# A new order of all engines' work, and loads issued tensor by tensor, in a recurrence with a maxout network behind it

## The chip, the cores and the metric

The kernel runs on one core of one Trainium2 chip. The metric is the device time of a run in microseconds (us); lower is better. A core has five engines with a queue of instructions each: PE (TensorE, matrix products), DVE (VectorE), ACT (ScalarE), POOL (GpSimd) and SP (SyncE, here used only to issue transfers). Each engine works through its own queue in order; an instruction whose inputs are not ready holds up everything behind it on that engine. Transfers between HBM and the on-chip memory SBUF are moved by 16 DMA engines. PE writes its products to PSUM, which has eight banks.

## The reference

Two parts follow each other. The first is a gated linear recurrence over 768 positions for 4 batches and 8 heads of size 48; the second is a network with a maximum of three products.

```python
for t in range(S):                       # S = 768, state is 48 x 48 per batch and head
    state = alpha[:, :, t, :, None] * state + np.einsum('bhd,bhe->bhde', k[:, :, t], v[:, :, t])
    y[:, :, t] = np.einsum('bhd,bhde->bhe', q[:, :, t], state)
# x: y as 3072 rows of 384
h = np.maximum(np.maximum(x @ w1, x @ w2), x @ w3)     # 384 x 768 each
out = h @ w_out                                        # 768 x 384
```

## The kernel before

The 768 positions are cut into six blocks of 128, and two batches are handled together: that makes 12 steps (0 to 11), each of 256 rows of the network. A step holds two units u (one batch each). Steps 0 and 1 are the first block of the two pairs of batches and have no state from before; steps 10 and 11 are the last block and hand no state on.

A step is written as small pieces, each a letter with an index. The pieces of one step, in the order in which data flow:

- a load of alpha, k, q and v, 384 KB each, by SP (L87), into rings of four buffers: step s + 4 reuses the buffer of step s. Weights are loaded by SP as well, in 12 parts w0 to w11 of 384 KB (L99, L102), and cast by W0 to W11 (on POOL at L140, on ACT at L138).
- N: logarithm of alpha (ACT, L168). c: sums of it by a product with a triangle (PE, L175, L178). e, f, g: exponentials of the sums (ACT, L184, L190, L196). k, q: inputs times these (POOL or DVE, L203). V: v scaled and cast (ACT, L144).
- T: transposes of q and k, eight a unit (PE, L221); t: their copy (DVE L140 or ACT L138). A: scores (PE, L235); a: scores times the mask (DVE, L248), four a step. Y: attend (PE, L271), in strips of 32 columns; x: its copy, the network's input (L138 or L140).
- S: the state's product (PE, L292); s: its sum with the old state (DVE, L304); M: gate products (POOL, L282, L284); z: the decay of the state (POOL or DVE, L309).
- G0 to G8: the network's products, six instructions of 256 columns each (PE, L322). G with index i needs weight part wi. h0 to h8: copy or maximum (h0, h3, h6 copy on ACT or DVE, L138 or L140; the others are maxima on DVE, L337). O: the output product, six of 384 columns (PE, L346); O2 to O5 are its halves, four and two products. o: scaling of the output (L144 or L146) and its store by SP (L354).
- H: fillers, products of a blank tile, which keep PE busy before the inputs have arrived (PE, L359).

What order these take is written out by hand in three strings: PROLOGUE (emitted once, with the pieces of steps 0 to 2 and the front of 3 and 4), STEADY (emitted for steps 3 to 10, in which the network of step s, the attention of step s + 1 and the sums of step s + 2 lie side by side) and LAST (step 11). "O0@-1" is piece O0 of the step before, "N0@2" piece N of the step after next. A letter behind the index names the engine (v DVE, p POOL, a ACT) or, for PE's pieces, the pool of PSUM banks that its result takes: w has two banks, s two, g four, and each pool's banks are handed out in turn, so that a piece waits until the bank's last result has been read. Each engine's queue holds its pieces in the order of the strings; nothing is reordered later.

```python
    for i, item in enumerate(LOADS.split()):       # L109: the first 28 loads, in this order
        ...
    with tc.manual_schedule():                     # L411
        ...
        emit(0, PROLOGUE)
        for s in range(3, NS):
            emit(s, LAST if s == NS - 1 else STEADY)
```

Of the kernel before, what the change touches and what calls it, by code (L numbers as in the profile page):

```python
# [23 lines left out]
def kernel(  # L24
# [14 lines left out]
    B, H, S, D = q.shape  # L39
# [42 lines left out]
    def where(s):  # L82
        return s // (B // U), (s % (B // U)) * U

    def load(n, s):
        cb, b0 = where(s)
        nc.sync.dma_start(  # L87
            rings[n][s % NQ],
            ins[n][b0:b0 + U, :, cb * P:(cb + 1) * P].rearrange("b h s d -> s (b h) d"))

    def load_step(s, *_):
        for n in "akqv":
            load(n, s)

    def load_weight(i):
        if i < 9:
# [6 lines left out]

    c16 = cpool.tile([P, 3 * P + 2], FP16, name="c16")
    c32 = cpool.tile([P, 4], FP32, name="c32")
    LOADS = """a1 a0 q0 w0 k0 k1 q1 w2 v0 a2 v1 w1
        w3 w4 w6 w5 q2 k2 w7 w8 v2 a3 w11 w10
        w9 q3 k3 v3"""
    for i, item in enumerate(LOADS.split()):  # L109
        if item[0] == "w":  # L110
            load_weight(int(item[1:]))
# [5 lines left out]
    tri, w2 = c16[:, :P], c16[:, P:P + 2]  # L117
# [8 lines left out]
    def clear_padding():  # L126
        for i in range(NQ):
            for t, eng in ((las[i], nc.vector), (qks[i], nc.gpsimd), (vts[i], nc.vector)):
                eng.memset(t.rearrange("p a b c -> p (a b) c")[:, :, D:], 0.0)
# [226 lines left out]
    def warm(_, n, *x):  # L356
# [3 lines left out]

    every, kept = NS, NS - B // U
    pieces = {
        "L": (load_step, every), "W": (cast_weight, every), "H": (warm, every), "N": (logs, every),
        "c": (sums, every), "e": (decay_in, every), "f": (decay_out, every), "g": (totals, every),
        "k": (scale_k, every), "q": (scale_q, every), "V": (values, every),
        "T": (turn, every), "t": (keep_turned, every), "A": (scores, every), "a": (masked, every),
# [5 lines left out]
    def emit(s, order):  # L372
        for piece in order.split():
            piece, _, at = piece.partition("@")
            fn, end = pieces[piece[0]]
            step = s + int(at or "0")
            if 0 <= step < end:
                i = piece[1:].rstrip("vpags")
                fn(step, int(i or 0), piece[1 + len(i):])

    PROLOGUE = """N0@1 H5@0 H2@0 H2@0 H3@0 H5@0 H1@0 H6@0 N0@0 c1@0 c0g@0 f1@0
        H4@0 c1@1 q1p@0 g0@0 f0@0 e1@0 e0@0 H4@0 q0v@0 H2@0 k1v@0 k0p@0
        c0g@1 H2@0 f0@1 q0p@1 e0@1 e1@1 T1@0 T0g@0 t1a@0 f1@1 t0@0 g0@1
        H2@0 W0a@0 H3@0 A0g@0 A1@0 H6@0 a0@0 a2@0 V0@0 a1@0 a3@0 k0p@1
        k1v@1 H2@0 H2@0 T0@1 N0@2 L0@4 H2@0 q1p@1 T1g@1 Y0@0 Y1@0 t0@1
        A0@1 H2@0 t1@1 x0v@0 x1@0 V0@1 W2p@0 A1g@1 S1@0 a0@1 a1@1 a3@1
        c1@2 G0@0 e1@2 c0@2 f0@2 H2@0 a2@1 f1@2 S0@0 e0@2 Y0g@1 g0@2
        h0v@0 Y1g@1 W3a@0 s1a@0 W1p@0 W6p@0 G1@0 x1v@1 x0v@1 W4a@0 G2@0 h1@0
        s0@0 G0@1 h0@1 S1@1 G1@1 G3@1 h2@0 S0@1 M0@0 h1@1 W5a@0 s0@1
        G3@0 z0p@0 z1p@0 q1p@2 G4@0 G2@1 h3@0 h3v@1 L0@5 G4@1 h4@0 q0v@2  # L390
        h2@1 G6@0 G5@1 k1p@2 k0v@2 T0@2 h4@1 s1a@1 T1g@2 h6@0 t0a@2 W7p@0
        h5@1 t1@2 G5@0 G6@1 W8a@0 A0g@2 A1@2 h5@0 a0@2 G7@0 h6@1 W11p@0
        G8@0 G7@1 W10p@0 a1@2 W9p@0 V0@2 a2@2 a3@2 Y0@2 h7@1 N0@3 Y1@2
        G8@1 c1@3 x0@2 h7@0 h8@0 c0@3 h8@1 x1@2 f0@3 f1@3 G0@2 G1@2
        G2@2 q1p@3 e0@3 G3@2 q0p@3 h0@2 h3@2 h1@2 h2@2 G4@2 g0@3 k0p@3
        O0@0 e1@3 o0v@0 M0@1 L0@6 G6@2 h4@2 O1@0 k1v@3 G5@2 o1@0 h6v@2
        T0@3 t0a@3 T1g@3 O0@1 h5@2 t1@3 o0v@1 A0@3 V0@3 A1g@3 z0p@1 a2@3
        O1g@1 a3@3 a0@3 a1@3 N0@4 c1g@4 G7@2 o1@1 g0@4 z1p@1 G8@2 M0@2
        e1@4 h7@2 c0g@4 k1p@4 f1@4 f0@4 e0@4 Y0@3 Y1g@3 q0p@4 q1v@4 h8@2
        x0@3 x1@3 V0@4 k0v@4"""  # L400
    STEADY = """S1@-1 S0g@-1 N0@2 T1@1 t1@1 s0@-1 s1@-1 O0@-1 T0@1 G0@0 t0@1 G3@0
        z0v@-1 A1@1 a2@1 A0g@1 z1p@-1 O1@-1 o0v@-1 h0@0 a0@1 c0@2 h3@0 G1@0
        c1g@2 e0@2 a1@1 f0@2 G2@0 a3@1 e1@2 g0@2 G4@0 k1p@2 o1@-1 Y0@1
        h1@0 h2@0 h4@0 f1@2 q0p@2 k0p@2 V0@2 Y1@1 G5@0 h5@0 x0@1 G6@0
        q1p@2 x1@1 G7@0 L0@4 h6v@0 h7@0 G8@0 M0@0 h8@0"""
    LAST = """G0@0 G3@0 h0@0 G1@0 h1@0 h3@0 G2@0 G6@0 h2@0 h6@0 G7@0 G5@0
        G4@0 G8@0 h7@0 O0@-1 h4@0 h5@0 h8@0 O1g@-1 o0v@-1 O4g@0 O5@0 O2g@0
        o1@-1 O3@0 o1v@0 o0@0"""

    blank = cpool.tile([P, 512], FP16, name="blank")  # L410
    with tc.manual_schedule():  # L411
        nc.vector.memset(blank, 0.0)  # L412
        clear_padding()
# [4 lines that stand above are left out]
# [29 lines left out]
```

## Time and profile before

| | |
|---|---|
| median of 5 runs | 159.64 us (159.06 to 160.28) |
| the profiled execution, time | 159.64 us |
| its span, first to last instruction | 157.9 us |
| granted PE clock, mean | 0.996 |
| busy: PE, DVE, ACT, POOL | 150.7, 126.6, 78.7, 62.0 us |
| transfers | 28.73 MB, mean 182 GB/s |
| first piece of the first steady step (S1@2) starts | 54.17 us |
| the last step's PE work (LAST) begins | 144.6 us |
| last output product ends | 154.45 us |

Times in the text are microseconds from the span's start. In a list of instruction groups a line reads: line of the code, engine, operation, output<-input with shapes and types, number of instructions, busy time and mean duration in ns, and the idle time of the engine just ahead of them with what ended it. A timeline's line reads: start, length, engine, line, operation, tiles, shapes, number of instructions merged, and in brackets the idle time ahead and what ended it. PE's instructions overlap each other: what one costs is the time from its start to the next start, and its listed length is longer.

### The profile page before, as it was taken

The numbers are of one execution on the slowest core, as the hardware profiler recorded it, in microseconds if no ns is written. First come the engines' busy times: TensorE is split into PE (matmuls) and PEld (weight loads), VectorE is DVE, ScalarE is ACT, GpSimd is POOL, SyncE is SP. The second block draws the span as 40 slices with busy tenths as digits, with TensorE's granted clock in tenths as the row PEclk, the third lists the DMA queues.
The fourth block names the chain that finished last, engine by engine and source line by source line (L and its number), as shares of the span: only waits on it lengthen the run. The fifth ranks groups of instructions, "written<-read, shape, count | busy, mean of one in ns | idle before, by whom it ended". The sixth has DMA issues, their size and how long they took to land.

```text
span 157.9 us, 4886 instructions
## 1 busy us (share of the span) xinstructions
PE 150.7 (95%) x2057; PEld 115.1 (73%) x2057; DVE 126.6 (80%) x210; ACT 78.7 (50%) x153; POOL 62.0 (39%) x87
## 2 busy tenths in 40 slices
PE   6999998979998999999999999999999999999991
PEld 2355667868865777878878878878878879778860
DVE  3024997799667799899898998998998998998570
ACT  3447368557636739628329249059067164222211
POOL 5024802950585623724625427328319219200000
PEclk9999999999999999999999999999999999999998
DMA  5999999999899999999899999999981011020014
GB/s 121 214 262 247 183 269 338 202 294 282 223 198 211 222 172 240 209 235 303 179 228 218 224 220 226 228 232 218 229 183 56 0 50 54 0 104 2 4 50 150
DMA packets 107254, 28.73 MB, mean 182 GB/s; under 512 B 99808, under 2 KB 107232, under 8 KB 107232
## 3 DMA queue, kind: packets, MB, share of 16 engines
q1 hardware_dynamic: 106944, 28.32, 81.9%
q8 instruction: 16, 0.26, 0.7%
q10 hardware_dynamic: 288, 0.10, 0.2%
q14 instruction: 6, 0.05, 0.1%
HBM read 23.69 MB, written 4.72 MB: 180 GB/s over the span
## 4 chain that ended last, share of the span: by engine, by line
PE 67%; SPq 13%; DMA 8%; DVE 5%; ACT 3%; issue 1%
PE gps L322 39%; PE ops L346 12%; SPq L87 9%; PE yps L271 5%; PE tps L221 4%; DMA ws<-in_moe_w_dram 4%; SPq L99 4%; DMA ra<-in_alpha_dram 4%; PE aps L235 3%; PE lps L175 2%; DVE qk L203 2%; PE sps L292 2%; ACT h L138 1%; PE lps L178 1%; DVE hT L337 1%
## 5 line engine op out<-in xcount | busy, mean ns | idle before, releaser
L322 PE MATMUL gps<-xT,wcat 128*128 128x256 f16 x648 | 77.8, 273 | 0.8 <-POOL wcat L140 0.6
L322 PEld LDWEIGHTS <-wcat 128*128 128x128 f16 x648 | 61.3, 98 | 10.1 <-POOL wcat L140 0.8
L248 DVE TENSOR_TENSOR lat<-aps,c 128x512 f16<-128x512 f32 x48 | 30.6, 683 | 0.8 <-PE aps L235 0.7
L138 ACT CAST h<-gps 128x512 f16<-128x512 f32 x25 | 14.5, 586 | 32.7 <-PE gps L322 32.1
L203 POOL TENSOR_TENSOR qk<-rk,ic 128x384 f16<-128x384 f32 x19 | 19.8, 1041 | 25.4 <-ACT ge L196 20.8
L337 DVE TENSOR_TENSOR h<-gps,h 128x512 f16<-128x512 f32 x36 | 24.6, 685 | 5.8 <-ACT h L138 2.6
L337 DVE TENSOR_TENSOR hT<-gps,h 128x512 f16<-128x512 f32 x36 | 24.7, 690 | 5.4 <-PE gps L322 3.3
L346 PE MATMUL ops<-wo,hT 128*128 128x384 f16 x144 | 26.9, 326 | 0.0
L203 POOL TENSOR_TENSOR qk<-rq,ac 128x384 f16<-128x384 f32 x21 | 21.4, 1023 | 10.6 <-ACT ge L196 7.4
L346 PEld LDWEIGHTS <-hT 128*128 128x128 f16 x144 | 13.0, 98 | 7.8 <-issue 0.2
L309 POOL TENSOR_TENSOR st<-full,gm 128x384 f16<-128x384 f32 x12 | 9.9, 830 | 20.7 <-DVE full L304 20.6
L359 PE MATMUL wps<-blank 128*128 128x512 f16 x57 | 16.3, 433 | 1.2 <-DVE blank L412 1.2
L140 DVE COPY qkT<-tps 128x1024 f16<-128x1024 f16 x21 | 14.3, 683 | 2.2 <-PE tps L221 2.2
L184 ACT ACTIVATE ic<-lps 128x384 f32<-128x384 f32 x24 | 11.6, 493 | 8.6 <-PE lps L175 7.6
L221 PE MATMUL tps<-c,qk 128*128 128x128 f16 x192 | 14.5, 219 | 1.3 <-DVE qk L203 0.8
L168 ACT ACTIVATE la<-ra 128x768 f16<-128x768 f32 x12 | 10.3, 860 | 10.8 <-DMA ra<-in_alpha_dram 10.8
L221 PEld LDWEIGHTS <-qk 128*128 128x128 f16 x192 | 12.0, 97 | 3.5 <-DVE qk L203 1.2
L190 ACT ACTIVATE ac<-lps 128x384 f32<-128x384 f32 x24 | 11.6, 495 | 4.2 <-PE lps L175 2.5
L144 ACT ACTIVATE vt<-rv,c 128x768 f16<-128x768 f32 x12 | 11.4, 946 | 4.3 <-DMA rv<-in_v_dram 4.3
L359 PEld LDWEIGHTS <-blank 128*128 128x128 f16 x57 | 5.8, 109 | 8.2 <-issue 3.3
L144 ACT ACTIVATE ob<-ops,c 128x384 f32<-128x384 f32 x12 | 7.0, 584 | 8.8 <-PE ops L346 8.8
L271 PE MATMUL yps<-lat,vt 128*32 128x128 f16 x384 | 10.3, 219 | 0.0
(37 smaller groups left out, 141.0 us busy)
## 6 DMA issues: line engine op xcount, KB each, us to landing
ra<-in_alpha_dram SPq DMA_DIRECT2D x12, 384.0 KB, 4.9
rq<-in_q_dram SPq DMA_DIRECT2D x12, 384.0 KB, 5.9
rk<-in_k_dram SPq DMA_DIRECT2D x12, 384.0 KB, 5.8
rv<-in_v_dram SPq DMA_DIRECT2D x12, 384.0 KB, 6.0
out_dram<-ob SPq DMA_DIRECT2D x24, 192.0 KB, 2.6
ws<-in_moe_w_dram SPq DMA_DIRECT2D x9, 384.0 KB, 5.0
ws<-in_moe_w_out_dram SPq DMA_DIRECT2D x3, 384.0 KB, 6.2
c<-c ACTq DMA_DIRECT2D x1, 96.5 KB, 3.0
```

The source lines that it names most:

```text
L87: nc.sync.dma_start(rings[n][s % NQ], ins[n][b0:b0 + U, :, cb * P:(cb + 1) * P].rearrange("b h s d -> s (b h) d"))
L138: nc.scalar.copy(out=dst, in_=src)
L140: engines[eng].tensor_copy(out=dst, in_=src)
L144: nc.scalar.mul(dst, src, col)
L203: engines[eng or "p"].tensor_mul(dst.rearrange("p a b c -> p (a b) c")[:, :, :D], src[:, u * H:(u + 1) * H], dec)
L221: nc.tensor.transpose(tps[:, i, p, :], qk[:, u * NP + i * HP + p].rearrange("p a b -> p (a b)"), ident)
L248: nc.vector.tensor_mul(lat, aps_of[s, u][i], m)
L271: nc.tensor.matmul(yps[C * c:C * (c + 1), f, :], job[n][0], job[n][1], start=(n == 0), stop=(n == len(job) - 1))
L322: nc.tensor.matmul(gps[:, j, :], wcat[:, f, g, jj * P:(jj + 1) * P], xT[:, f].rearrange("p u t -> p (u t)"), start=(f == 0), stop=(f == NF ...
L337: nc.vector.tensor_max(h, gps, h_of[s, i - 1])
L346: nc.tensor.matmul(ops, hT_of[s][:, jj, u * P:(u + 1) * P], wo16[:, jj, :], start=(jj == 0), stop=(jj == NJ - 1))
L359: nc.tensor.matmul(wps, blank[:, :P], blank, start=True, stop=True)
```

## The change

All three order strings and the order of the first loads are new. Loads of later steps, which were one piece L that issued alpha, k, q and v, become four pieces l0 to l3 that issue one tensor each. The pieces themselves, the tiles, the banks and the buffers are unchanged; which engine or bank pool a piece uses is changed for some of them by its letter. In STEADY, the copy t1 goes from DVE to ACT, h0 from ACT to DVE, h6 from DVE to ACT, the decay z0 from DVE to POOL, k0 from POOL to DVE, V from ACT to DVE; the scores' pair A0 A1, the attend pair Y0 Y1 stay adjacent on PE, O0 goes to the front of the step, and the loads go ahead of the store of o1.

```diff
--- before.py
+++ after.py
@@ -88,9 +88,8 @@
             rings[n][s % NQ],
             ins[n][b0:b0 + U, :, cb * P:(cb + 1) * P].rearrange("b h s d -> s (b h) d"))
 
-    def load_step(s, *_):
-        for n in "akqv":
-            load(n, s)
+    def load_step(s, i, _):
+        load("akqv"[i], s)
 
     def load_weight(i):
         if i < 9:
@@ -103,9 +102,9 @@
 
     c16 = cpool.tile([P, 3 * P + 2], FP16, name="c16")
     c32 = cpool.tile([P, 4], FP32, name="c32")
-    LOADS = """a1 a0 q0 w0 k0 k1 q1 w2 v0 a2 v1 w1
-        w3 w4 w6 w5 q2 k2 w7 w8 v2 a3 w11 w10
-        w9 q3 k3 v3"""
+    LOADS = """a0 a1 k0 q0 q1 k1 v0 v1 a2 w0 w1 w3
+        w2 k2 q2 w4 w6 w5 w7 w8 v2 a3 w10 w9
+        w11 q3 k3 v3"""
     for i, item in enumerate(LOADS.split()):
         if item[0] == "w":
             load_weight(int(item[1:]))
@@ -360,7 +359,7 @@
 
     every, kept = NS, NS - B // U
     pieces = {
-        "L": (load_step, every), "W": (cast_weight, every), "H": (warm, every), "N": (logs, every),
+        "l": (load_step, every), "W": (cast_weight, every), "H": (warm, every), "N": (logs, every),
         "c": (sums, every), "e": (decay_in, every), "f": (decay_out, every), "g": (totals, every),
         "k": (scale_k, every), "q": (scale_q, every), "V": (values, every),
         "T": (turn, every), "t": (keep_turned, every), "A": (scores, every), "a": (masked, every),
@@ -378,34 +377,35 @@
                 i = piece[1:].rstrip("vpags")
                 fn(step, int(i or 0), piece[1 + len(i):])
 
-    PROLOGUE = """N0@1 H5@0 H2@0 H2@0 H3@0 H5@0 H1@0 H6@0 N0@0 c1@0 c0g@0 f1@0
-        H4@0 c1@1 q1p@0 g0@0 f0@0 e1@0 e0@0 H4@0 q0v@0 H2@0 k1v@0 k0p@0
-        c0g@1 H2@0 f0@1 q0p@1 e0@1 e1@1 T1@0 T0g@0 t1a@0 f1@1 t0@0 g0@1
-        H2@0 W0a@0 H3@0 A0g@0 A1@0 H6@0 a0@0 a2@0 V0@0 a1@0 a3@0 k0p@1
-        k1v@1 H2@0 H2@0 T0@1 N0@2 L0@4 H2@0 q1p@1 T1g@1 Y0@0 Y1@0 t0@1
-        A0@1 H2@0 t1@1 x0v@0 x1@0 V0@1 W2p@0 A1g@1 S1@0 a0@1 a1@1 a3@1
-        c1@2 G0@0 e1@2 c0@2 f0@2 H2@0 a2@1 f1@2 S0@0 e0@2 Y0g@1 g0@2
-        h0v@0 Y1g@1 W3a@0 s1a@0 W1p@0 W6p@0 G1@0 x1v@1 x0v@1 W4a@0 G2@0 h1@0
-        s0@0 G0@1 h0@1 S1@1 G1@1 G3@1 h2@0 S0@1 M0@0 h1@1 W5a@0 s0@1
-        G3@0 z0p@0 z1p@0 q1p@2 G4@0 G2@1 h3@0 h3v@1 L0@5 G4@1 h4@0 q0v@2
-        h2@1 G6@0 G5@1 k1p@2 k0v@2 T0@2 h4@1 s1a@1 T1g@2 h6@0 t0a@2 W7p@0
-        h5@1 t1@2 G5@0 G6@1 W8a@0 A0g@2 A1@2 h5@0 a0@2 G7@0 h6@1 W11p@0
-        G8@0 G7@1 W10p@0 a1@2 W9p@0 V0@2 a2@2 a3@2 Y0@2 h7@1 N0@3 Y1@2
-        G8@1 c1@3 x0@2 h7@0 h8@0 c0@3 h8@1 x1@2 f0@3 f1@3 G0@2 G1@2
-        G2@2 q1p@3 e0@3 G3@2 q0p@3 h0@2 h3@2 h1@2 h2@2 G4@2 g0@3 k0p@3
-        O0@0 e1@3 o0v@0 M0@1 L0@6 G6@2 h4@2 O1@0 k1v@3 G5@2 o1@0 h6v@2
-        T0@3 t0a@3 T1g@3 O0@1 h5@2 t1@3 o0v@1 A0@3 V0@3 A1g@3 z0p@1 a2@3
-        O1g@1 a3@3 a0@3 a1@3 N0@4 c1g@4 G7@2 o1@1 g0@4 z1p@1 G8@2 M0@2
-        e1@4 h7@2 c0g@4 k1p@4 f1@4 f0@4 e0@4 Y0@3 Y1g@3 q0p@4 q1v@4 h8@2
-        x0@3 x1@3 V0@4 k0v@4"""
-    STEADY = """S1@-1 S0g@-1 N0@2 T1@1 t1@1 s0@-1 s1@-1 O0@-1 T0@1 G0@0 t0@1 G3@0
-        z0v@-1 A1@1 a2@1 A0g@1 z1p@-1 O1@-1 o0v@-1 h0@0 a0@1 c0@2 h3@0 G1@0
-        c1g@2 e0@2 a1@1 f0@2 G2@0 a3@1 e1@2 g0@2 G4@0 k1p@2 o1@-1 Y0@1
-        h1@0 h2@0 h4@0 f1@2 q0p@2 k0p@2 V0@2 Y1@1 G5@0 h5@0 x0@1 G6@0
-        q1p@2 x1@1 G7@0 L0@4 h6v@0 h7@0 G8@0 M0@0 h8@0"""
-    LAST = """G0@0 G3@0 h0@0 G1@0 h1@0 h3@0 G2@0 G6@0 h2@0 h6@0 G7@0 G5@0
-        G4@0 G8@0 h7@0 O0@-1 h4@0 h5@0 h8@0 O1g@-1 o0v@-1 O4g@0 O5@0 O2g@0
-        o1@-1 O3@0 o1v@0 o0@0"""
+    PROLOGUE = """N0@0 N0@1 H2@0 H9@0 H2@0 H2@0 H1@0 H3@0 H2@0 c0@0 c1@1 c1g@0
+        e1@0 f1@0 H2@0 k1p@0 f0@0 H3@0 q1v@0 g0@0 e0@0 H1@0 H1@0 T1@0
+        H1@0 q0v@0 H1@0 k0p@0 c0g@1 g0@1 f1@1 H4@0 e1@1 f0@1 t1@0 q1v@1
+        H2@0 q0v@1 e0@1 T0@0 H4@0 k0p@1 H2@0 A1g@0 a2@0 k1p@1 T0g@1 T1@1
+        t0a@0 V0@0 a3@0 t0@1 t1a@1 l0@4 l1@4 l2@4 l3@4 A0g@0 N0@2 a0@0
+        H4@0 W3p@0 W1p@0 W6p@0 A1g@1 W5p@0 a1@0 A0@1 a2@1 a0@1 a1@1 H2@0
+        a3@1 S1@0 S0@0 H1@0 s1@0 H5@0 c1@2 V0@1 Y0g@1 W0v@0 Y0@0 Y1g@1
+        c0@2 x0@0 x1v@1 S1g@1 x0@1 s0a@0 Y1g@0 l0@5 l1@5 l2@5 l3@5 x1v@0
+        f0@2 s1@1 g0@2 G0@1 h0v@1 H3@0 W7p@0 G0@0 h0@0 G1@1 e1@2 M0@0
+        W8p@0 W2v@0 G3@0 G1@0 h1@1 f1@2 e0@2 k1v@2 k0v@2 G2@0 h1@0 h3@0
+        S0@1 W4a@0 q1v@2 q0v@2 G3@1 G2@1 z0p@0 z1p@0 W9p@0 W11p@0 h2@0 T1@2
+        h3@1 t1a@2 T0@2 h2@1 G4@0 G4@1 h4@0 G6@0 t0a@2 h4@1 G6@1 s0@1
+        A1@2 G5@1 h6v@1 h6@0 G5@0 V0@2 a3@2 a2@2 h5@1 h5@0 G7@0 A0@2
+        G8@0 a0@2 G7@1 a1@2 h7@0 Y1@2 Y0@2 x0@2 x1v@2 N0@3 h8@0 G8@1
+        G0@2 G1@2 c1@3 h7@1 h0@2 h8@1 g0@3 h1@2 G2@2 c0@3 f0@3 e0@3
+        e1@3 W10p@0 G6@2 q0p@3 M0@1 G4@2 G3@2 h2@2 f1@3 h3@2 h4@2 G5@2
+        q1v@3 h6@2 k0v@3 h5@2 k1p@3 O0@0 O0g@1 T0@3 t0a@3 T1g@3 z1p@1 o0v@1
+        V0@3 t1@3 l0@6 l1@6 l2@6 l3@6 O1@0 o1@0 A1@3 A0g@3 G8@2 o0v@0
+        O1@1 a3@3 a1@3 N0@4 G7@2 a2@3 c1@4 a0@3 h7@2 z0p@1 o1v@1 c0g@4
+        f1@4 h8@2 Y1@3 Y0g@3 g0@4 M0@2 e0@4 f0@4 e1@4 x1v@3 q0v@4 k0v@4
+        q1p@4 x0@3 V0@4 k1v@4"""
+    STEADY = """O0@-1 S1g@-1 G0@0 s1@-1 G1@0 S0@-1 T0@1 T1@1 h0v@0 t0@1 h1@0 o0v@-1
+        G3@0 G6@0 t1a@1 s0@-1 A0g@1 N0@2 A1@1 h3@0 O1@-1 h6@0 z1p@-1 a1@1
+        z0p@-1 G2@0 a0@1 G4@0 c0g@2 l0@4 l1@4 l2@4 l3@4 a2@1 h2@0 h4@0
+        a3@1 c1@2 G7@0 e0@2 G8@0 k0v@2 e1@2 G5@0 f1@2 f0@2 h7@0 g0@2
+        q1p@2 o1@-1 Y0@1 Y1g@1 x0@1 q0p@2 k1p@2 x1@1 h5@0 h8@0 V0v@2 M0@0"""
+    LAST = """O0@-1 G0@0 G3@0 h3v@0 G4@0 G5@0 h4@0 h0@0 G6@0 h6@0 G1@0 h5@0
+        G7@0 G2@0 h1@0 h7@0 h2@0 G8@0 h8@0 O1@-1 O4g@0 o1@-1 O5g@0 O2g@0
+        o0v@-1 O3@0 o1@0 o0@0"""
 
     blank = cpool.tile([P, 512], FP16, name="blank")
     with tc.manual_schedule():
```

## The prediction

> **What bounds the kernel now.** I read the page first, then a table of stages, then the matrix engine's (PE) timeline, then the waits on loads. The profiled execution took 159.64 us, which is also the median; its span is 157.9 us, so 1.74 us lie around the span. All sums below are made against this execution.
>
> ```profile
> PE 150.7 (95%) x2057; PEld 115.1 (73%) x2057; DVE 126.6 (80%) x210; ACT 78.7 (50%) x153; POOL 62.0 (39%) x87
> ...
> q8 instruction: 16, 0.26, 0.7%
> ...
> L359 PE MATMUL wps<-blank 128*128 128x512 f16 x57 | 16.3, 433 | 1.2 <-DVE blank L412 1.2
> ```
>
> PE is busy for 95% of the span, and 57 of its instructions are fillers on a blank tile. The table of stages, two steady steps and the last stretch (columns: stretch, length, busy time and count of PE, PEld, DVE, ACT, POOL, granted clock, DMA share, GB/s):
>
> ```profile
> 77.55:88.81 11.26, 11.26 (x176) 9.15 (x174) 10.49 (x18) 6.06 (x13) 5.08 (x8) 1.00 1.09 225
> 88.81:100.07 11.26, 11.26 (x176) 9.15 (x174) 10.49 (x18) 5.78 (x12) 5.08 (x8) 1.00 1.10 223
> 144.60:157.90 13.30, 9.81 (x79) 7.39 (x76) 6.24 (x10) 2.92 (x5) 0.00 (x0) 0.95 0.17 60
> ```
>
> A steady step is 11.26 us of PE with nothing idle, at full clock; DVE has 0.77 us to spare in it. Is anything hidden in those 11.26 us? The PE timeline of a step, read by differences of starts:
>
> ```profile
> 102.12 1.47 PE L322 MATMUL gps<-xT,wcat 128*128 128x256 f16 x12
> 103.53 0.62 PE L235 MATMUL aps<-qkT 48*128 48x128 f16 x16
> 104.08 1.15 PE L346 MATMUL ops<-wo,hT 128*128 128x384 f16 x6
> ...
> 108.55 2.79 PE L322 MATMUL gps<-xT,wcat 128*128 128x256 f16 x24
> 111.18 0.50 PE L292 MATMUL sps<-vt,qk 128*128 128x96 f16 x8
> ```
>
> 24 gate products take 111.18 - 108.55 = 2.63 us, 0.109 each. The 12 ahead of the scores take 1.41, 0.10 more than 12 x 0.109: the change of array shape. There are four such changes in a step (into and out of scores, into and out of attend), 0.4 us. No other hole shows. So only the prologue, up to the first steady step at 54.17, has waits to lose.
>
> ```profile
> 32.32 0.39 PE L221 MATMUL tps<-c,qk 128*128 128x128 f16 x4
> 33.51 0.84 PE L221 MATMUL tps<-c,qk 128*128 128x128 f16 x12 [0.80 <-DVE qk L203]
> ...
> 47.01 0.39 PE L221 MATMUL tps<-c,qk 128*128 128x128 f16 x4
> 47.78 0.84 PE L221 MATMUL tps<-c,qk 128*128 128x128 f16 x12 [0.39 <-POOL qk L203]
> ```
>
> Four transposes last 4 x 0.057 = 0.23, so the first pair of lines hides 33.51 - 32.55 = 0.96 us, the second 47.78 - 47.24 = 0.54. By the same reading the other losses are 0.5 (15.1), 0.3 (21.2), 0.77 (23.9), 0.2 (43.5), 0.28 (51.0) in the prologue, 0.25 (54.5) and 0.31 (59.8) in the first steady step: about 4 us. That is the most that any order could win, since the change keeps all work.
>
> What holds the prologue's end is the loads. Timelines of ACT, DVE and POOL:
>
> ```profile
> 46.31 0.56 DVE L203 TENSOR_TENSOR qk<-rk,ic 128x384 f16<-128x384 f32 x1 [0.17 <-DMA rk<-in_k_dram]
> ...
> 46.35 1.38 POOL L203 TENSOR_TENSOR qk<-rk,ic 128x384 f16<-128x384 f32 x1 [0.15 <-DMA rk<-in_k_dram]
> ...
> 50.45 0.84 ACT L168 ACTIVATE la<-ra 128x768 f16<-128x768 f32 x1 [0.39 <-DMA ra<-in_alpha_dram]
> ...
> 58.80 0.84 ACT L168 ACTIVATE la<-ra 128x768 f16<-128x768 f32 x1 [1.98 <-DMA ra<-in_alpha_dram]
> ```
>
> k of step 3 lands at 46.3, alpha of step 4 at 50.4, alpha of step 5 at 58.8, and the stages above show a DMA share of 1.0 and more. The queue is the limit, so the nth load lands when it does whatever the engines' order.
>
> **The change: what stays.** I counted the pieces of both orders: prologue, steady step and last step hold the same pieces, 57 fillers included. Steady PE work and its four changes of shape are the same (A0 A1 adjacent, Y0 Y1 adjacent). So are the last step's 54 gate and 24 projection products; it moves O0@-1 ahead of the gates, 6 x 0.163 us, a shift within PE. I cost it at nothing: h8@0 still has O1 and O4 (0.97 + 0.65 us) to hide behind, of which it needs about 0.9. The last output still goes over ACT (0.58) and then its store. Loads split by tensor stay a, k, q, v in a row on SP: the split itself is 0. In a steady step they now stand ahead of the store of o1 rather than behind it; the DMA share is full until 118 us, and a steady step asks for its alpha some 3 us after landing (94.9 against 98.1, step 9), so 0.
>
> **The first loads.** The 20 first loads are the same set in both orders and the 8 after them end q3 k3 v3 in both, with only weights w9 to w11 turned. So k3 at 46.3 and a4 at 50.4 stay. Within the 20, attention's inputs come earlier (v1 about 17.0 in place of 22.2, by 1.7 us a load) and w0 at about 20.3 in place of 9.8.
>
> **The front, to G0@1.** PE: fillers start at 1.19, 12 of them cold until 6.28, 9 more at 0.215 to 8.21; sums 0.90, 7 fillers 1.5: 10.6. T1@0 waits for q1@0: q0 lands at about 10.1, DVE shares the multiply's time with POOL's k1@0 (as at 10.4 now, 1.00 us) and ends at 11.3: 0.7 us lost. Then T 0.46, 2 fillers, c 0.16, 6 fillers, T 0.46, 6 fillers: scores A1g@0 at 15.4. From there DVE is the chain: from 15.9 eight masks and one transposed copy at 0.61 each, 0.2 us of waiting for A1g@1 in between, to 21.65; s1@0 0.5; cast W0v, new on DVE, between 0.4 (half its time on ACT, 0.84) and 0.9, I take 0.8, the near row; x1@1 0.5: G0@1 starts at 23.6.
>
> **To the k3 gate.** From G0@1 to T0@3 PE has 25 gate pieces x 0.655 = 16.4, 3 fillers 0.65, S 0.17, T@2 0.91, A@2 apart and so with two more changes of shape 0.96, Y@2 1.0, c@3 0.53, O0 twice 1.95: 22.6 us, hence 46.15. I held each gate against its weight: G4@0 at 30.6 (w4 at 28.9 + 0.84), G8@0 at 36.1 (w8 at 34.7 + 0.83), Y1@2 at 37.4 (v2 at 36.45 + 0.94, a tenth late). The 0.96 us before T@2 goes, since k2 and q2 land some 4 us earlier. But now k3 decides: k0v@3 on DVE is done at 46.87, k1p@3 on POOL at 47.73 (the two rows above are this very pair). T0@3 goes at 46.9, T1g@3 at 47.8. What was won ahead, up to 1.2 us, is waited away here.
>
> **From the gate to the first steady step.** After 47.8: T1 0.46, O1@0 0.97, A@3 0.65, G8@2 0.66, O1@1 0.97, G7@2 0.66, c@4 0.53, Y@3 1.0: 5.9, so 53.7. Now it takes from 47.78 to 54.17. a4 does not bind: its logarithm ends at 51.3, c1@4 comes at 52.2. Gain **0.47**.
>
> **First steady step.** N@5 stands ahead of h3@3 and h6@3 on ACT. If a5 lands at 58.8, h3 ends at 60.25 and G2@3, due at 60.15, is 0.1 late. On DVE x1@3, q0@4, k0@4, k1@4 and s1 push h1@3 to about 59.0; A0g@4, due at 58.65, needs its bank: 0.3. Together 0.4, where now 0.56 are lost: gain 0.16.
>
> **Steady steps.** DVE gives up t1 (0.6) and z0 (0.83) and takes k0 (0.56 alone, 1.21 beside POOL) and V (0.4 to 0.9). I walked it from step start: h1 4.5 (needed by A0g at 4.94), o0 5.0 (O1 at 5.49), a0 6.8 (c0g at 7.78), k0v 9.14, h7 9.70, h5 10.41, h8 11.02 to 11.71. The next O0, now first in the step, reads h8's half in its fifth product at 11.27 + 0.65 = 11.92. Cover 0.15 us: nothing lost. Here a rule of the Trainium skill speaks against the change: SBUF — State Buffer, section "SBUF: two separate sides", says that a vector operation with two SBUF inputs and a GpSimd operation hold a common port pair exclusively, the later one blocked to the end. The 1.38 us on POOL beside DVE's 0.56 above (1.00 alone) agrees in kind. By the rows, k0v starts at 9.14, ahead of POOL's q1 at 9.4, and takes 0.56: sum 0. By the rule with POOL first, k0v waits up to 1.0, less the cover: up to 0.85 us in each of seven steps, 6 us. I take the row, since q1p waits for f1, which ACT makes after e0. V is last on DVE; if blocked behind k1p for 1.0 it still ends before t0 is due.
>
> **Sum.** -0.47 - 0.16 + 0 = -0.63: 159.64 - 0.63 = **159.0 us**.
>
> **Rivals and chances.** Within 0.5% (158.84 to 160.44) counts as no change, about what a measurement of this kernel can tell. (A) As above, 158.4 to 159.5, chance 0.45; two fifths of it below 158.84. (B) The gates ease: k3 half a microsecond sooner, no loss in the first steady step, 159.0 - 0.5 - 0.4 = 158.1; for it, alpha 5's late landing is one row; against it, the full DMA share; 0.20. (C) The front slips by more than the 1.2 us of slack at k3, DVE's row of masks being the place; 1.5 us beyond the slack would give 160.5, a small slip about 159.6; 0.17, a third of it slower. (D) Slower: h8 comes after O0's fifth product in every step, by DVE's k0v beside POOL. It decides from 0.15 us on; at 1.21 us for k0v it costs 0.65 - 0.15 = 0.5 in seven steps, 3.5 us: 162.5; 0.18. That PE's fetches matter and the new order frees them, I count in B: 16 blocks are moved and no hole in a step answers to them. Faster 0.18 + 0.20 = 0.38, same 0.27 + 0.12 = 0.39, slower 0.05 + 0.18 = 0.23. The range, 157.9 to 161.5, takes in B and C and D's lower part.
>
> **What would show it.** T1g@3 of the new profile resumes near 47.8 after POOL; the first steady O0@2 near 53.7; steady steps 11.26 us with O0 unbroken; G0@1 near 23.6. I am wrong if a steady step is longer than 11.3, if k3 lands elsewhere than 46 to 46.7, or if PE reaches T0@3 after 47.3.

## The result, and the profile after

The changed kernel took 158.74 us (median of 28 runs, 158.27 its lowest) against 159.79 us before (49 runs). The ratio is 0.9948, 95% interval 0.9931 to 0.9965: a gain of 0.83 us, 0.56 to 1.10. I had said 159.0 us, a gain of 0.63. On two other occasions the same kernel was set beside the one before and the ratio was 0.9919 (0.9892 to 0.9946) and 0.9900 (0.9852 to 0.9948), gains of 1.3 and 1.6 us: the gain is real. The three intervals overlap, so that it was larger on those occasions is not shown.

The profile that came with the result ran at a granted clock of 0.855 and a span of 172.5 us, so the profiles read here are those of the same kernel at full clock from the experiments: run 11 (span 156.6 us), unless another is named. Stages of it, two steady steps and the last stretch, in the columns used above (PE, PEld, DVE, ACT, POOL, granted clock, DMA share, GB/s):

```profile
77.29:88.56 11.27, 11.27 (x177) 9.16 (x175) 10.68 (x18) 5.76 (x12) 5.40 (x8) 1.00 0.99 204
88.56:99.82 11.26, 11.26 (x176) 9.16 (x174) 10.68 (x18) 5.76 (x12) 5.39 (x8) 1.00 1.03 221
143.20:156.60 13.40, 9.97 (x86) 7.55 (x78) 5.69 (x9) 3.52 (x7) 0.00 (x0) 1.00 0.16 60
```

A steady step is 11.26 us of PE as before: the new order gains nothing there. DVE is at 10.68 rather than 10.49 us. Next comes the gate at k3, by which I mean the place where PE can go no further until k of step 3 has landed (a "gate piece" is something else, one of G0 to G8). The timelines of PE, DVE and POOL there:

```profile
46.51 1.13 PE L220 MATMUL tps<-c,qk 128*128 128x128 f16 x12
47.87 0.40 PE L220 MATMUL tps<-c,qk 128*128 128x128 f16 x4 [0.24 <-POOL qk L202]
...
46.40 0.56 DVE L202 TENSOR_TENSOR qk<-rk,ic 128x384 f16<-128x384 f32 x1 [0.53 <-DMA rk<-in_k_dram]
...
46.51 1.30 POOL L202 TENSOR_TENSOR qk<-rk,ic 128x384 f16<-128x384 f32 x1 [1.13 <-DMA rk<-in_k_dram]
```

PE comes to the transposes at 46.5, k3 lands at 46.4, DVE's multiply ends at 46.96, POOL's at 47.81, and the last four transposes go at 47.87. Sixteen transposes need 0.91 us and take from 46.51 to 48.11: 0.69 us are waited away. What follows, in PE's timeline (the first steady step) and DVE's:

```profile
53.57 1.14 PE L345 MATMUL ops<-wo,hT 128*128 128x384 f16 x6
54.54 0.33 PE L291 MATMUL sps<-vt,qk 128*128 128x96 f16 x4
54.77 1.47 PE L321 MATMUL gps<-xT,wcat 128*128 128x256 f16 x12
56.07 0.33 PE L291 MATMUL sps<-vt,qk 128*128 128x96 f16 x4
56.24 1.06 PE L220 MATMUL tps<-c,qk 128*128 128x128 f16 x16
57.14 1.47 PE L321 MATMUL gps<-xT,wcat 128*128 128x256 f16 x12
58.54 0.62 PE L234 MATMUL aps<-qkT 48*128 48x128 f16 x16
...
64.87 1.15 PE L345 MATMUL ops<-wo,hT 128*128 128x384 f16 x6
...
54.49 0.70 DVE L202 TENSOR_TENSOR qk<-rq,ac 128x384 f16<-128x384 f32 x1
55.12 1.01 DVE L202 TENSOR_TENSOR qk<-rk,ic 128x384 f16<-128x384 f32 x2
56.06 0.54 DVE L303 TENSOR_TENSOR full<-sps,st 128x384 f32<-128x384 f32 x1
56.52 0.67 DVE L139 CAST h<-gps 128x512 f16<-128x512 f32 x1
57.12 0.67 DVE L139 COPY qkT<-tps 128x1024 f16<-128x1024 f16 x1
57.72 0.67 DVE L336 TENSOR_TENSOR h<-gps,h 128x512 f16<-128x512 f32 x1
```

The first steady step starts at 53.57 (54.17 before) and has no wait worth naming on PE: each row begins where the row ahead of it has issued its last product, and only 0.06 us are lost at S1. The next step starts at 64.87, so this one took 11.30 us. In the profile of before PE's timeline of the first steady step, up to the start of the next, has

```profile
54.17 0.51 PE L292 MATMUL sps<-vt,qk 128*128 128x96 f16 x8
54.77 0.62 PE L221 MATMUL tps<-c,qk 128*128 128x128 f16 x8
...
58.06 0.72 PE L235 MATMUL aps<-qkT 48*128 48x128 f16 x16
58.71 1.15 PE L346 MATMUL ops<-wo,hT 128*128 128x384 f16 x6
59.69 0.33 PE L175 MATMUL lps<-la,c 128*128 128x384 f16 x1
60.16 0.81 PE L322 MATMUL gps<-xT,wcat 128*128 128x256 f16 x6
...
66.11 0.50 PE L292 MATMUL sps<-vt,qk 128*128 128x96 f16 x8
```

and took 66.11 - 54.17 = 11.94 us: 0.25 are lost ahead of T1, 0.1 within the scores and 0.31 ahead of a gate piece.

Where did the 1.24 us between the two spans (157.86 and 156.62) come from? 0.60 are gained by the start of the first steady step (54.17 against 53.57) and 0.64 within that step (11.94 against 11.30). Behind it nothing changed: from the second steady step to the last product's start it is 154.08 - 66.11 = 87.97 us before and 152.84 - 64.87 = 87.97 now, and from there to the span's end both take 3.78.

### The profile page after: what moved, and what is told of

Read it like the earlier page. It is cut to its first block, busy times and chain, and to the rows that moved or that the text cites. A ratio compares the mean times of both kernels' runs of the same rounds, so it can differ in the third digit from the quotient of the medians.

```text
span 172.5 us, 4881 instructions
## 1 busy us (share of the span) xinstructions
PE 167.4 (97%) x2057; PEld 122.2 (71%) x2057; DVE 130.1 (75%) x215; ACT 77.9 (45%) x150; POOL 60.3 (35%) x85
## 4 chain that ended last, share of the span: by engine, by line
PE 91%; DMA 3%; SPq 2%; DVE 1%; ACT 0%; issue 0%; DVEq 0%
PE gps L321 47%; PE ops L345 17%; PE tps L220 7%; PE yps L270 6%; PE wps L358 4%; PE aps L234 4%; DMA rq<-in_q_dram 3%; PE lps L174 2%; SPq L87 2%; PE sps L291 2%; PE lps L177 1%; DVE qk L202 1%; ACT ob L143 0%; DVEq L202 0%
## 5 line engine op out<-in xcount | busy, mean ns | idle before, releaser
L321 PE MATMUL gps<-xT,wcat 128*128 128x256 f16 x648 | 88.2, 294 | 0.0
L321 PEld LDWEIGHTS <-wcat 128*128 128x128 f16 x648 | 65.1, 103 | 14.5
L345 PE MATMUL ops<-wo,hT 128*128 128x384 f16 x144 | 30.4, 355 | 0.0
L137 ACT COPY qkT<-tps 128x1024 f16<-128x1024 f16 x13 | 13.1, 1013 | 32.5 <-PE tps L220 32.5
L308 POOL TENSOR_TENSOR st<-full,gm 128x384 f16<-128x384 f32 x20 | 16.9, 847 | 28.8 <-DVE full L303 23.7
L202 POOL TENSOR_TENSOR qk<-rq,ac 128x384 f16<-128x384 f32 x16 | 16.5, 1049 | 26.6 <-ACT ac L189 26.6
L137 ACT CAST xT<-yps 128x384 f16<-128x384 f32 x20 | 9.2, 482 | 14.7 <-PE yps L270 14.7
L202 POOL TENSOR_TENSOR qk<-rk,ic 128x384 f16<-128x384 f32 x12 | 12.0, 1003 | 9.4 <-ACT ic L183 7.2
L139 DVE COPY qkT<-tps 128x1024 f16<-128x1024 f16 x11 | 7.6, 688 | 5.5 <-PE tps L220 5.5
L202 DVE TENSOR_TENSOR qk<-rq,ac 128x384 f16<-128x384 f32 x8 | 5.6, 725 | 8.1 <-DMA rq<-in_q_dram 8.1
```

The lines of the kernel that those rows point to most:

```text
L137: nc.scalar.copy(out=dst, in_=src)
L202: engines[eng or "p"].tensor_mul(dst.rearrange("p a b c -> p (a b) c")[:, :, :D], src[:, u * H:(u + 1) * H], dec)
L308: engines[eng or "p"].tensor_mul(sts[b0 + u][(cb + 1) % 2].rearrange("p a (b d) -> p a b d", d=D), full_of.pop((s, u)), gm_of[s][:, u * HP ...
L321: nc.tensor.matmul(gps[:, j, :], wcat[:, f, g, jj * P:(jj + 1) * P], xT[:, f].rearrange("p u t -> p (u t)"), start=(f == 0), stop=(f == NF ...
L345: nc.tensor.matmul(ops, hT_of[s][:, jj, u * P:(u + 1) * P], wo16[:, jj, :], start=(jj == 0), stop=(jj == NJ - 1))
```

## The experiments

All ratios are against the kernel before, run on the same chip. Runs 1 to 4, 5 to 8 and 9 to 11 went together, and medians are compared within such a group or through these ratios.

**1, the changed kernel as it is.**

> The changed kernel as it is, for a profile at full clock. Both theories: about 0.8 us under the kernel before. Load gate: T1g@3 resumes at 47.8 after POOL's k1@3, the first steady O0@2 starts near 53.7, steady steps are 11.26 us. Steady order (rival): the first steady step starts near 54.2 as before and the gain comes behind it.

Measured: 159.05 us, ratio 0.9919 (0.9892 to 0.9946). k3 landed at 46.94, 0.56 us later than in run 11; the last four transposes of T1@3 went on at 48.43, and the first steady step started at 54.13, not at 53.7. Shift these by the late landing and they stand about where they were expected. But from there on PE lost only 0.06 us. So both answers were half right in this execution: with a late k3 the start is no sooner than in the old profile, and the gain lies behind it.

**2 and 3, the two halves alone.** Run 2 has the new LOADS and PROLOGUE (together the new front) with the old STEADY and LAST; run 3 the reverse.

```diff
 # run 2: changed kernel, with
+    STEADY = """S1@-1 S0g@-1 N0@2 T1@1 t1@1 s0@-1 s1@-1 O0@-1 T0@1 G0@0 ...   (old)
+    LAST = """G0@0 G3@0 h0@0 G1@0 h1@0 ...   (old)
 # run 3: changed kernel, with
+    LOADS = """a1 a0 q0 w0 k0 k1 q1 w2 v0 a2 v1 w1 ...   (old)
+    PROLOGUE = """N0@1 H5@0 H2@0 H2@0 H3@0 ...   (old)
```

> New LOADS and PROLOGUE, old STEADY and LAST. Load gate: 0.5 to 0.8 us under the kernel before, about the time of the changed kernel. Steady order: 0 against the kernel before.

> Old LOADS and PROLOGUE, new STEADY and LAST. Load gate: 0 to 0.2 us under the kernel before. Steady order: 0.6 to 0.8 us under it.

Measured: run 2 160.78 us, ratio 1.0046 (1.0018 to 1.0073); run 3 160.05 us, ratio 0.9979 (0.9952 to 1.0006). Neither theory had this: the new front alone is slower, the new steady order alone is not told apart from no change, both together gain 0.8%. The seam between them is the place. PE's timeline of run 2 at its first steady step:

```profile
55.21 0.50 PE L295 MATMUL sps<-vt,qk 128*128 128x96 f16 x8
56.42 0.40 PE L224 MATMUL tps<-c,qk 128*128 128x128 f16 x4 [0.72 <-POOL qk L206]
57.78 0.40 PE L224 MATMUL tps<-c,qk 128*128 128x128 f16 x4 [0.95 <-DVE qk L206]
58.01 1.14 PE L349 MATMUL ops<-wo,hT 128*128 128x384 f16 x6
```

The old step begins with T1@4 after 0.34 us, and the new front leaves k1 of step 4 to the end of DVE's queue: about 2.0 us are lost, 0.87 ahead of the first transposes (56.42 - 55.55) and 1.13 between the eight of them (58.01 - 56.42, less the 0.46 that they need). In run 3 the new step begins with O0, and the old front leaves h8@2 behind q1@4 on DVE:

```profile
55.17 0.82 PE L349 MATMUL ops<-wo,hT 128*128 128x384 f16 x4
56.54 0.50 PE L349 MATMUL ops<-wo,hT 128*128 128x384 f16 x2 [0.54 <-DVE hT L340]
```

O0's fifth product waits for h8, 0.72 us. That is the kind of wait that the slower rival (D) of the prediction had in each step, here once at the seam; its cause is another, h8's place in DVE's queue and not a k0v held up by POOL. Later steps are 11.27 us in both runs.

**4, five more fillers ahead of c1@2.**

```diff
-H1@0 s1@0 H5@0 c1@2
+H1@0 s1@0 H10@0 c1@2
```

> The changed kernel with five more fillers (1.07 us of PE) ahead of c1@2. Load gate: PE reaches T0@3 up to 1.2 us ahead of k3, so 0 to 0.3 us over the changed kernel. Rival, PE's own work sets the end of the prologue: 1.07 us over it.

Measured: 159.17 us, ratio 0.9936 (0.9904 to 0.9969), 0.12 us over run 1, which is not told apart from none. It tells less than I had meant: the fillers went into a wait that stood just there (0.41 + 0.47 us in run 1, for alpha 2 and for V1 behind it), so PE came to G0@1 at 24.21 as in run 1 (24.25), and the slack at k3 was not touched.

**5, the kernel before once more.**

> The kernel before once more, for a second profile beside those of the changed kernel, to see how far a load's landing moves from one execution to the next. Load gate: T1 and T0 of step 3 resume within 0.6 us after k3 lands, wherever that is, and the first steady step loses 0.5 to 1 us. Rival (the order alone sets it): the first steady step starts at 54.2 again whatever k3 does.

Measured: 160.8 us in this one execution, span 159.0. The first steady step starts at 55.12, not 54.17, and takes 12.15 us, 0.9 more than a later one; 0.78 of that is a wait at T1@4. k3 landed at 47.28, but PE did not wait for it: alpha 3, late at 40.6, had held PE already. PE's timeline of this run, and that of run 6, which has the new front and an alpha 3 as late (40.4):

```profile
39.44 0.83 PE L322 MATMUL gps<-xT,wcat 128*128 128x256 f16 x6
41.51 0.32 PE L175 MATMUL lps<-la,c 128*128 128x384 f16 x1 [1.25 <-ACT la L168]
```

```profile
39.82 2.14 PE L321 MATMUL gps<-xT,wcat 128*128 128x256 f16 x18
41.80 0.33 PE L174 MATMUL lps<-la,c 128*128 128x384 f16 x1
```

The old order has c1@3 behind one gate piece (G8@1) and waits; the new one has G0@2 and G1@2 between and does not. My expectation that k3 would rule the old kernel as well was wrong for this execution. It doesn't follow that the new front fares better with late loads: in run 6 k3 landed at 48.10 and the first steady step started at 55.29, no sooner than here.

**6, the transposes early in the steady step.**

```diff
-O0@-1 S1g@-1 G0@0 s1@-1 G1@0 S0@-1 T0@1 T1@1 h0v@0
+O0@-1 S1g@-1 T0@1 T1@1 G0@0 s1@-1 G1@0 S0@-1 h0v@0
```

> The changed kernel with the transposes T0@1 T1@1 of the steady step moved ahead of G0 G1 S0, near where the old order has them. If the gain is the late place of the transposes in the first steady step: 0.9 to 1.1 us over the changed kernel, all of it in the first steady step, waiting for q and k of step 4 on DVE; later steps 11.26 us. Rival (their place doesn't matter): 0.

Measured: 160.0 us, ratio 0.9963 (0.9932 to 0.9995), where run 7 beside it, equal to the changed kernel in time, has 0.9918 (0.9891 to 0.9945): by the ratios some 0.7 us lost, though the intervals just overlap. The profile decides it: it has 0.49 + 0.25 us of waiting for DVE's q and k in the first steady step, which takes 12.02 us instead of 11.30, and a later one takes 11.27. This move alone gives back more than half of the gain.

**7, five more fillers behind G0@1.**

```diff
-G0@1 h0v@1 H3@0 W7p@0
+G0@1 h0v@1 H8@0 W7p@0
```

> The changed kernel with five more fillers (1.07 us of PE) between G0@1 and G0@0, behind the wait for alpha 2 that took in the five of the earlier run. Load gate at k3: PE reaches T0@3 at 47.7 rather than 46.7 and waits the less: 0 to 0.3 us over the changed kernel. Rival, PE's work sets the end: 1.07 us over it.

Measured: 159.25 us, ratio 0.9918. Against run 1 (0.9919) the 1.07 us of PE work cost nothing that shows; the ratio is good to 0.4 us. PE's timeline at the gate, with k3 at 47.10:

```profile
47.02 0.39 PE L220 MATMUL tps<-c,qk 128*128 128x128 f16 x4
47.74 0.62 PE L220 MATMUL tps<-c,qk 128*128 128x128 f16 x8 [0.34 <-DVE qk L202]
48.59 0.40 PE L220 MATMUL tps<-c,qk 128*128 128x128 f16 x4 [0.23 <-POOL qk L202]
```

With 1.07 us more work ahead of it PE still waits 0.5 us and then 0.4 here, though k3 also came 0.7 us later than in run 11.

**8 and 9, k3 loaded first.** Both load q3 and k3 ahead of the output weight, cast that weight behind k1@3 on POOL and put the output products behind the scores; run 9 also mends two places in DVE's queue. Stretches left out are marked by dots.

```diff
 # run 8
-v2 a3 w10 w9 w11 q3 k3 v3
+v2 a3 q3 k3 w10 w9 w11 v3
-q1v@3 h6@2 k0v@3 h5@2 k1p@3 O0@0 O0g@1 T0@3 t0a@3 T1g@3 ... A1@3 A0g@3 G8@2 ... O1@1 ... G7@2
+q1v@3 h6@2 k0v@3 h5@2 k1p@3 W10p@0 W9p@0 W11p@0 T0@3 t0a@3 T1g@3 ... G7@2 h7@2 G8@2 h8@2
+V0@3 A1@3 A0g@3 a3@3 a1@3 a2@3 a0@3 O0@0 O0g@1 o0v@0 ... O1@0 O1@1 o0v@1 N0@4 c1@4 o1@0
 # run 9, besides
-f1@3 h3@2 h4@2 G5@2 q1v@3 h6@2 k0v@3 h5@2
+f1@3 k0v@3 q1v@3 h3@2 h4@2 G5@2 h6@2 h5@2
-a3@3 a1@3 a2@3 a0@3 O0@0 O0g@1 o0v@0
+a3@3 a1@3 O0@0 o0v@0 a2@3 a0@3 O0g@1
```

> The changed kernel with q3 and k3 loaded ahead of the three parts of the output weight, and T, G7, G8, A of step 3 ahead of the four output products that need these. Load gate: k3 lands near 43.5, the waits at T@3 (1.1 us) go, the first steady step starts near 53.1: 0.6 to 1.0 us under the changed kernel. Rival (another gate, alpha 4 or q4 k4, stands just behind): 0 to 0.3 us under it.

Measured: 161.83 us, ratio 1.0077 (1.0052 to 1.0102). k3 landed at 42.5, four us sooner, and T@3 waited longer than ever. PE's timeline, and DVE's:

```profile
47.51 0.84 PE L220 MATMUL tps<-c,qk 128*128 128x128 f16 x12 [2.50 <-DVE qk L202]
...
44.79 0.69 DVE L336 TENSOR_TENSOR h<-gps,h 128x512 f16<-128x512 f32 x1 [2.05 <-ACT h L137]
45.40 0.97 DVE L202 TENSOR_TENSOR qk<-rq,ac 128x384 f16<-128x384 f32 x1
46.29 1.17 DVE L202 TENSOR_TENSOR qk<-rk,ic 128x384 f16<-128x384 f32 x1
```

h4@2 stood at the head of DVE's queue for 2.05 us waiting for ACT's h3; the multiplies were behind it, and then beside POOL's casts took 0.97 and 1.17 us, where the changed kernel has 0.55 and 0.56. (The profiled execution, at 160.91, is one of the faster ones: seven of the twelve had a mean clock of 0.989 instead of 0.997 and took 161.75 to 162.3. Where their clock fell is not on record, so part of the median's loss stays open.)

> As the run with k3 first, but k0 and q1 of step 3 moved on DVE ahead of h4@2, where DVE sat idle for 2.05 us waiting for ACT's h3, and o0@0 ahead of two masks. If that run lost its 2.7 us at T@3 to DVE's queue: T@3 runs without a wait, the first steady step starts near 53.2, 0.5 to 1.0 us under the changed kernel. Rival (the loads set the end in some other place, alpha 4, q4 or alpha 5): the time of the changed kernel within 0.3 us.

Measured: 158.58 us, ratio 0.9888 (0.9841 to 0.9934), beside 158.92 and 0.9900 for run 11: the wait of 2.7 us is gone, which puts it down to DVE's queue, but the 0.3 us under the changed kernel is not told apart from none. Another wait took the gate's place:

```profile
44.65 0.83 PE L220 MATMUL tps<-c,qk 128*128 128x128 f16 x12
45.77 0.40 PE L220 MATMUL tps<-c,qk 128*128 128x128 f16 x4 [0.29 <-POOL qk L202]
```

0.45 us go to POOL's k1@3, which stands behind q0@3 and the gate products M on POOL, and the first steady step starts at 53.40, against 53.57 in run 11 and 53.2 expected.

**10, the old LOADS under the new order.** Only the list of loads is the old one.

```diff
-    LOADS = """a0 a1 k0 q0 q1 k1 v0 v1 a2 w0 w1 w3 w2 k2 q2 w4 w6 w5 w7 w8 ...
+    LOADS = """a1 a0 q0 w0 k0 k1 q1 w2 v0 a2 v1 w1 w3 w4 w6 w5 q2 k2 w7 w8 ...
```

> The changed kernel with the old LOADS. v1 lands 5 us later and attend of step 1 waits for it, weights 0, 1 and 2 come earlier. Load gate at k3, which stays in its place, with PE some 1 to 2 us ahead of it: 0 to 0.4 us over the changed kernel. Rival (the earlier inputs of the attention are the gain): 0.8 us or more over it.

Measured: 166.45 us, ratio 1.0355 (1.0304 to 1.0405). I had looked at v1 alone. It cost 0.9 us, as G0@1 came at 24.97 against 24.07 in run 11; most of the rest is one wait for q2 and k2 and the slower clock behind it. PE's and DVE's timelines, and two stages (columns as above):

```profile
35.78 1.89 PE L220 MATMUL tps<-c,qk 128*128 128x128 f16 x16 [4.60 <-DVE qk L202]
37.47 4.61 PE L321 MATMUL gps<-xT,wcat 128*128 128x256 f16 x24
...
32.99 1.03 DVE L202 TENSOR_TENSOR qk<-rk,ic 128x384 f16<-128x384 f32 x2 [4.52 <-DMA rk<-in_k_dram]
```

```profile
30.00:35.00 5.00, 1.19 (x11) 0.81 (x9) 2.01 (x4) 0.34 (x2) 0.51 (x1) 0.94 0.80 215
35.00:40.50 5.50, 4.71 (x31) 3.85 (x32) 3.27 (x6) 2.24 (x3) 3.54 (x6) 0.50 1.09 264
```

The new order wants T@2 at 31, k2 lands at 32.9, and DVE's queue stands behind it. The loads and the order depend on each other.

**11, the changed kernel again.**

> The changed kernel once more, on the same chip as these two, as their measure. Load gate: T0@3 resumes within 0.7 us after k3 lands, as in its first profile, and the first steady step loses under 0.1 us wherever k3 lands. Rival (the first steady step was spared by luck of one execution): 0.4 us lost in it.

Measured: 158.92 us, and the profile shown at the head. k3 at 46.38; the transposes start at once, but wait 0.3 and 0.4 us within, and the last four go on 1.5 us after the landing, when POOL's multiply is done: the 0.7 us that I expected held for T0 alone. The first steady step loses 0.06 us in both profiles of this kernel and in run 7, with k3 at 46.38, 46.94 and 47.10, so it was not the luck of one execution.

## Why the prediction was right or wrong

**Total.** 159.0 said, 158.74 measured; the ratio said was 0.9960, measured 0.9948 (0.9931 to 0.9965). The sign and the two places of the gain held. The size is in part luck: the 0.63 us lie within the first comparison's interval, but below those of the other two (0.87 to 1.73 and 0.83 to 2.37 us), and the profiles give 1.24. One term of the sum was too small, that of the first steady step.

**What stays, and the steady step.** Held: 11.26 us, four changes of shape. The cover of h8 came out as worked: in step 7 h8 ended at 110.43, the next O0 began at 109.93 and its fifth product at 109.93 + 0.65 = 110.58, 0.15 us later. k0v took 0.55 us, the row's value: it started ahead of POOL, so the rule of the Trainium skill (SBUF — State Buffer, "SBUF: two separate sides") did not reach it. V starts just behind POOL's k1, and there the trace agrees with the rule:

```profile
110.35 1.34 DVE L145 TENSOR_SCALAR vt<-rv,c 128x768 f16<-128x768 f32 x1
...
110.25 1.01 POOL L202 TENSOR_TENSOR qk<-rk,ic 128x384 f16<-128x384 f32 x1
```

V took 1.34 us, not 0.4 to 0.9, and ended 0.43 us after POOL had; in the other six steps it ended 0.41 to 0.43 us after. No run has V on DVE with POOL idle, so what it takes alone is not shown. As predicted for that case it cost nothing, since t0 comes later.

**The front.** G0@1 came at 23.50 to 24.25 in the seven profiles that have the new front unchanged up to there (all but run 4), where 23.6 was said (the terms of that sum add up to 23.4). The sum had DVE's row of masks as the chain, and that is not what decided: in all seven G0@1 starts 3.32 to 3.33 us after ACT begins the logarithm of alpha 2, because c1@2, and V1 behind N@2 on ACT, wait for it. In run 11, on ACT and on PE:

```profile
20.75 0.84 ACT L167 ACTIVATE la<-ra 128x768 f16<-128x768 f32 x1 [2.27 <-DMA ra<-in_alpha_dram]
21.50 0.92 ACT L143 ACTIVATE vt<-rv,c 128x768 f16<-128x768 f32 x1
...
22.47 0.85 PE L270 MATMUL yps<-lat,vt 128*32 128x128 f16 x48 [0.33 <-ACT vt L143]
...
24.07 0.81 PE L321 MATMUL gps<-xT,wcat 128*128 128x256 f16 x6
```

The prediction doesn't name alpha 2 there. By its 1.7 us a load, one place behind v1, it would have landed at 18.7; it landed at 20.2 to 20.9. The slack ahead of k3 took that in, and it was about as large as said: in run 11 PE waits 0.69 us at the transposes and had come 0.47 late to G0@1, together 1.16 against 1.2.

**The gate at k3.** Held, and more exactly than any single profile shows. The traces of nine runs have the landing of k3 (DVE's multiply starts 0.02 or 0.03 us after it wherever DVE waits for it) and the start of the first steady step:

| run | front | k3 lands | first steady step starts | between |
|---|---|---|---|---|
| before | old | 46.22 | 54.17 | 7.95 |
| 5 | old | 47.28 | 55.12 | 7.84 |
| 3 | old | 47.35 | 55.17 | 7.82 |
| 11 | new | 46.38 | 53.57 | 7.19 |
| 1 | new | 46.94 | 54.13 | 7.19 |
| 4 | new | 47.05 | 54.24 | 7.19 |
| 7 | new | 47.10 | 54.28 | 7.18 |
| 2 | new | 48.02 | 55.21 | 7.19 |
| 6 | new | 48.10 | 55.29 | 7.19 |

With the new front the start follows the landing by the same 7.19 us, with or without fillers (runs 4 and 7), and a late landing is passed on in full: the spans of runs 11, 1, 4 and 7 are 156.6, 157.2, 157.3 and 157.3 us. With the old front it is 7.8 to 8.0, though in run 5 alpha 3 and not k3 held PE. Two of my signs of being wrong did occur, k3 outside 46 to 46.7 in five of these six and PE at T0@3 after 47.3 in two (runs 2 and 6); they moved the start and left the mechanism. From the last transposes (47.87, where 47.8 was said) to the first steady step it took 5.70 us where 5.9 was said: I had put all eight transposes of T1 behind POOL's multiply, and only four stand there. The old order has twelve behind it (47.78) and then lost 0.28 us waiting for alpha 4, which is how it needs 6.39. Gain 0.60 against 0.47 said.

**The first steady step.** This term was mis-sized: 0.4 us of loss said, 0.06 measured in three profiles. The row of DVE did not push h1@3 to 59.0: POOL's q1@4 started at 53.78, DVE came to q0@4 at 54.49, was held up for little (0.70 us in place of 0.55), and h1@3 ended at 58.39, just ahead of the scores at 58.54. Alpha 5, which was to cost the other 0.1, landed at 58.33 instead of 58.8. The old order's loss there was larger than the 0.56 I had counted: 11.94 us against 11.27 for a later step is 0.67, since the scores lost 0.1 as well, and in run 5 it is 0.9. So this term is worth 0.64 us rather than 0.16, and 0.60 + 0.64 is the whole 1.24. That the late place of the transposes makes this gain is shown by run 6, which moves them forward and loses 0.72 us of it.

**What I had not counted** is how far k3's landing moves from one execution to the next. Between the two profiles of the sum it came 0.16 us later for the new kernel; at the same landing the gain would be 0.76 + 0.64 = 1.40 us, an estimate from the table and the two lengths of the first steady step. Whether the landing also explains why the three comparisons gave 0.8, 1.3 and 1.6 us was not tested.

**Rivals.** D, the slower one, did not come: k0v was not held up, and h8 had 0.15 us to spare. That a late h8 stops O0 at its fifth product is shown by run 3. B came half true: the first steady step lost nothing, k3 was no earlier. C did not show: the front slipped by up to 0.65 us and the slack held. Fetches of PE's instructions were not tested apart; every wait that the rows above mark has a load or another engine as its releaser, and no hole in a steady step is left for them.

## What to carry to other kernels

In a prologue that is fed by a full DMA queue, name the load that gates PE last: here work saved ahead of it was waited away, and fillers ahead of it cost nothing that showed. To test such a gate, set the time of its load beside the time of what it gates over several executions; a constant difference says more than one profile. A new order of the prologue, the order of its loads and the first pass of the loop behind it must be judged together: with the old loop, the old front or only the old loads left in, the ratios were 1.0046, 0.9979 and 1.0355, with all new 0.99. And a tensor that arrives sooner helps only if its consumer does not stand behind something slower in its own engine's queue (run 8).

## What the runs showed of the hardware

- In a wait of 4.6 us on PE (run 10) the granted clock fell, and it was 0.50 from 35.0 to 40.5: the four gate pieces behind the transposes took 42.00 - 37.47 = 4.53 us instead of 2.62. Behind a wait of 2.7 us (the profile of run 8) it stayed at 1.00.
- The same load lands at different times in two executions: k3 at 46.22 and 47.28 in the kernel before, at 46.38 and 46.94 in the changed one; alpha 3 at 38.2 and 40.6 in the kernel before.
- The cast of a weight part on DVE took 0.94 us with POOL idle (0.8 assumed from ACT's 0.84).
